# One prefill kernel on one core: a new bank for a piece of the early carry, and a new order for the first third of the tasks

## The chip, the cores and the metric

One core of a Trainium2 chip runs the whole program. The time is the device time of one execution in microseconds (us), as a median over runs. The core has five instruction streams that run beside each other and meet only at semaphores: TensorE (PE, matrix products), VectorE (DVE), ScalarE (ACT), GpSimd (POOL) and SyncE (SP, which here issues nearly all the transfers). Matrix products end in PSUM, which has eight banks; all other data lie in SBUF.

## The reference, cut to what matters

```python
def _attn_ref(q, k, v, alpha):            # each (4, 8, 768, 48)
    state = zeros((B, H, D, D))
    for t in range(S):
        state = alpha[:, :, t, :, None] * state + einsum('bhd,bhe->bhde', k[:, :, t], v[:, :, t])
        y[:, :, t] = einsum('bhd,bhde->bhe', q[:, :, t], state)

def _moe_ref(x, w_gate, w_val, w_out):    # x (3072, 384); weights (384,1536), (384,1536), (1536,384)
    g = x @ w_gate
    return (g * (1 / (1 + exp(-g))) * (x @ w_val)) @ w_out
```

The output of the first function, with the eight heads side by side in each row, is the `x` of the second.

## The kernel before, in words

**The two halves.** The recurrence is cut into 16 units of 192 positions, four to a batch, and the second half into seven blocks of tokens (384 or 512), each with 12 steps f over the hidden width. A step s is three long PE tasks: `g` (gate), `v` (value) and `o` (out). Each product is done with high and low parts of both factors, so `g` is nine matmuls. Block 0 needs the outputs of units 0 and 1, block 1 those of units 2 and 3. Steps 0 to 6 are block 0, steps 7 to 13 block 1 with the same weights.

**One unit.** Alpha, k and q arrive in rows (`La`, `Lk`, `Lq`). For the first four units they are copied into one of two wide buffers (`pa`, `pk`, `pq`, line 366), turned by PE into two PSUM banks (`Ta`, `Tk`, `Tq`, line 378) and taken from there (`ea`, `ek`, `cq`, line 927, or directly by the next multiplication). A backward running product of alpha (`G`, line 429) is multiplied by k (`mk`, line 953), a forward one (`f`, lines 433 and 436, in place in the single tile `AT`) by q (`q`, line 453 out of PSUM or 455 out of SBUF; `qc` copies a part of it, line 461). The keys are turned back (`K`, line 482; `kc`, lines 486 and 487), the scores are products of keys and queries (`S`, line 523), masked by `ma` (line 621). `Bw` (function `carry`, line 599) makes the state carried from chunk to chunk; `ad` copies it out (lines 635 and 642), `de` decays it into the next unit (line 650), `vc` copies values (line 468). `Y` (lines 693 to 710) gives the unit's output in two banks; `yh` and `yl` cut it into high and low parts (lines 724 and 728). For units 0 and 1 PE lays it out for the blocks (`R`, line 758; `x`, line 762); for the others ten to twelve transfers do (`xr`, line 775).

**Weights.** They come as 64-bit numbers in groups of one piece (groups 0 to 2) or two (all others): `wl` loads, `wNv0` to `wNv2` make single precision out of the words (lines 70 to 88), `wNa` and `wNp` make the high and low part (lines 291 and 295). Group 0 is the gate piece of step 0, group 1 its value piece, group 2 the gate of step 1, then in turn two of the list.

**The order.** Nothing is scheduled at run time. The string `ORDER` lists all tasks as `engine:name` (t PE, v DVE, s ACT, g POOL, y SP), with the PSUM banks of a task behind `@`. Each engine runs its own tasks strictly in this order, and waits at a task whose data, tile or bank is not yet free. A bank is free when the last reader of its former tile is done. The eight digits name A0, A1, A2, ops0, ops1, vps, gps, ops2; 6 is the bank of every `g` and 5 that of every `v`.

In `carry`, one piece of what is carried, `beside`, lies in the free columns of the first bank of the scores of the same unit:

```python
beside = st["S"][0][:, GF * T : GF * (T + D)].rearrange("p (g e) -> p g e", g=GF)
```

Of the kernel before, what the change touches and what calls it, by code (L numbers as in the profile page):

```python
# [28 lines left out]

WIDE = [(u + x, i) for u in range(0, NPE, 2) for x, i in ((0, 0), (1, 0), (0, 2), (0, 1), (1, 1), (1, 2))]  # L30
# [1229 lines left out]
```

## Time and profile before

| what | us |
|---|---|
| time of three runs, median | 550.85 |
| lowest and highest | 550.74, 550.98 |
| span of the profiled execution, first to last instruction | 549.9 |
| PE busy in it | 531.2 |
| start of the first `g` | 45.42 |

The profile is that of one execution. It shows its span; its own time with what lies around the span is not shown, and the median is 0.95 us longer than the span. Busy time is the time in which an engine runs an instruction; a row of a timeline has the start, the duration from the first to the last of the merged instructions, and in brackets how long the engine sat idle before and what ended the wait. The first 85 us matter here: before 45.42 us PE has only small tasks, and after it the long products run.

### The profile page before, as it was taken

How to read it: one execution, taken by the hardware profiler on the slowest of the kernel's cores; microseconds unless marked ns; L12 is line 12 of the kernel's file. 1: busy time of each engine (PE TensorE's matmuls, PEld its weight loads, DVE VectorE, ACT ScalarE, POOL GpSimd, SP SyncE). 2: the span in 40 equal slices, each digit the busy share in tenths (PEclk: the TensorE clock that was granted, in tenths of full speed). 3: DMA queues.
4: the chain of work that ended last, by engine and by line, in shares of the span. 5: the costliest groups of instructions: out<-in, count | busy, mean ns of one | idle time of the engine just before them, and what ended most of it. 6: DMA issues, size and time to landing. Idle time of an engine off the chain costs nothing.

```text
span 549.9 us, 13452 instructions
## 1 busy us (share of the span) xinstructions
PE 531.2 (97%) x5365; PEld 477.5 (87%) x5365; DVE 387.7 (71%) x619; ACT 264.1 (48%) x568; POOL 129.6 (24%) x139
## 2 busy tenths in 40 slices
PE   5879999999999999999999999999999999999995
PEld 3769999999999999998888888888888888899994
DVE  6989899998898997987789856476968353212122
ACT  5778754245334335423423513343335475447691
POOL 5454344142440122110202321012100030011011
PEclk9989999999999999999999999999999999999999
DMA  8889557574455656535464543546246434355321
GB/s 228 245 232 261 159 149 230 132 217 139 125 147 148 162 141 169 174 97 127 139 162 118 129 125 67 135 116 157 54 113 152 99 99 110 95 155 126 103 65 49
DMA packets 115111, 77.66 MB, mean 141 GB/s; under 512 B 53728, under 2 KB 111968, under 8 KB 115040
## 3 DMA queue, kind: packets, MB, share of 16 engines
q1 hardware_dynamic: 114192, 75.98, 51.9%
q8 instruction: 44, 0.72, 0.6%
q10 hardware_dynamic: 848, 0.74, 0.4%
q14 instruction: 27, 0.22, 0.2%
HBM read 62.52 MB, written 5.90 MB: 124 GB/s over the span
## 4 chain that ended last, share of the span: by engine, by line
PE 94%; DVE 2%; ACT 1%; DMA 1%; POOL 0%; issue 0%; DVEq 0%; POOLq 0%; ACTq 0%
PE g L791 27%; PE v L791 27%; PE ops L847 14%; PE ops L842 14%; PE y L680 3%; PE s L551 2%; PE A L599 1%; PE A L559 1%; PE pt L378 1%; PE kps L482 1%; DVE Gs L429 1%; DMA Le<-in_alpha_dram 1%; PE s L523 0%; ACT AT L927 0%; DVE t L78 0%; PE y L710 0%
## 5 line engine op out<-in xcount | busy, mean ns | idle before, releaser
L791 PE MATMUL g<-xT,w 128*128 128x384 f32 (+1 forms) x756 | 163.4, 360 | 0.0
L791 PE MATMUL v<-xT,w 128*128 128x384 f32 (+1 forms) x756 | 162.8, 359 | 0.0
L791 PEld LDWEIGHTS v<-xT,w 128*128 128x128 f32 x756 | 136.1, 188 | 13.2
L791 PEld LDWEIGHTS g<-xT,w 128*128 128x128 f32 x756 | 135.9, 188 | 13.2
L803 DVE TENSOR_TENSOR h<-h,v 128x384 f32<-128x384 f32 (+1 forms) x84 | 51.2, 609 | 110.6 <-PE v L791 94.3
L814 POOL TENSOR_TENSOR hl<-h,hh 128x384 fp32r<-128x384 f32 (+1 forms) x44 | 50.4, 1146 | 267.0 <-ACT hh L808 250.1
L799 ACT ACTIVATE h<-g 128x384 f32<-128x384 f32 (+1 forms) x84 | 45.0, 536 | 137.7 <-PE g L791 119.7
L808 ACT CAST hh<-h 128x384 fp32r<-128x384 f32 (+1 forms) x84 | 46.6, 555 | 77.6 <-PE ops L842 35.3
L847 PE MATMUL ops<-w,hh 128*128 128x384 f32 x286 | 79.6, 337 | 0.0
L842 PE MATMUL ops<-hh,w 128*128 128x512 f32 x216 | 72.2, 393 | 0.0
L498 DVE STREAM_TRANSPOSE K<-Gs 32x384 f32<-32x384 f32 x96 | 54.7, 570 | 2.0
L847 PEld LDWEIGHTS ops<-w,hh 128*128 128x128 f32 x286 | 52.2, 188 | 0.4
L842 PEld LDWEIGHTS ops<-hh,w 128*128 128x128 f32 x216 | 40.5, 188 | 8.9
L847 PE MATMUL ops<-w,hl 128*128 128x384 f32 x143 | 47.8, 335 | 0.0
L842 PE MATMUL ops<-hl,w 128*128 128x512 f32 x108 | 42.2, 391 | 0.0
L295 POOL TENSOR_TENSOR w<-t,w 128x768 fp32r<-128x768 f32 (+1 forms) x16 | 30.5, 1907 | 34.5 <-ACT w L291 30.8
L814 DVE TENSOR_TENSOR hl<-h,hh 128x384 fp32r<-128x384 f32 (+1 forms) x40 | 26.8, 670 | 8.9 <-ACT hh L808 8.6
L429 DVE TENSOR_TENSOR_SCAN Gs<-AT,Z 128x776 f32<-128x776 f32 x16 | 28.3, 1770 | 4.2 <-ACT AT L927 4.1
L436 DVE TENSOR_TENSOR_SCAN AT<-AT,Z 128x774 f32<-128x774 f32 x16 | 29.9, 1868 | 0.6
L261 ACT ACTIVATE wc<-wc 128x384 f32<-128x384 f32 x36 | 19.9, 553 | 15.6 <-DMA wc<-in_moe_w_gate_dram 8.1
L847 PEld LDWEIGHTS ops<-w,hl 128*128 128x128 f32 x143 | 26.9, 188 | 0.0
L621 DVE TENSOR_TENSOR X<-s,mask 128x384 f32<-128x384 f32 (+1 forms) x36 | 19.3, 552 | 8.6 <-PE s L551 8.1
(140 smaller groups left out, 695.2 us busy)
## 6 DMA issues: line engine op xcount, KB each, us to landing
xT<-X SPq DMA_DIRECT2D x72, 72.0 KB, 2.2
raw<-in_moe_w_gate_dram SPq DMA_DIRECT2D x12, 384.0 KB, 5.0
raw<-in_moe_w_val_dram SPq DMA_DIRECT2D x12, 384.0 KB, 6.2
V<-in_v_dram SPq DMA_DIRECT2D x96, 48.0 KB, 3.3
raw<-in_moe_w_out_dram SPq DMA_DIRECT2D x12, 384.0 KB, 4.7
wc<-in_moe_w_gate_dram SPq DMA_DIRECT2D x12, 384.0 KB, 3.7
wc<-in_moe_w_out_dram SPq DMA_DIRECT2D x12, 384.0 KB, 3.6
wc<-in_moe_w_val_dram SPq DMA_DIRECT2D x12, 384.0 KB, 4.2
```

The lines of the kernel that those rows point to most:

```text
L261: nc.scalar.activation(dev, dev, AF.Abs, accum_out=wviol[:, 1, i : i + 1])
L295: eng.tensor_tensor(out=lo, in0=src, in1=hi.bitcast(F32), op=ALU.subtract)
L429: nc.vector.tensor_tensor_scan(Gf[:, ::-1], Af[:, ::-1], Z[:, : 0 : -1], 0.0, op0=ALU.mult, op1=ALU.add)
L436: nc.vector.tensor_tensor_scan(Af, Af, Z[:, 1 : n + 1], Z[:, 0:1], op0=ALU.mult, op1=ALU.add)
L498: nc.vector.transpose(out=bass.AP(k0.tensor, k0.offset, [k0.ap[0], (G * 2 * D, NU), (2 * D, G), (1, 32)]), in_=Kg[j * BO + x : j * BO + x ...
L791: nc.tensor.matmul(pt, wsp[kind, f][a][:, kt * P : (kt + 1) * P], xT[blk][:, b_, kt, :], start=(n == 0), stop=(n == 3 * KT - 1),)
L799: nc.scalar.activation(h, acc.pop(("g", blk, f)), AF.Silu)
L803: nc.vector.tensor_tensor(out=h, in0=h, in1=acc.pop(("v", blk, f)), op=ALU.mult)
L808: nc.scalar.copy(out=hh, in_=acc["h", blk, f])
L814: eng.tensor_tensor(out=hl, in0=acc.pop(("h", blk, f)), in1=hh.bitcast(F32), op=ALU.subtract)
L842: nc.tensor.matmul(ops[blk][i], wsp["o", f][a][:, i * P : (i + 1) * P], h[b_], start=(first and n == 0), stop=(last and n == 2),)
L847: nc.tensor.matmul(ops[blk][i], h[b_][:, i * P : (i + 1) * P], wsp["o", f][a], start=(first and n == 0), stop=(last and n == 2),)
```

## The change

The order of the tasks is new from the start up to about step 41; from there on (about two thirds of the program) the string is the same. Engines change for some tasks, of which these matter here. From ACT to POOL go the wide copies `pa0`, `pk2`, `pa3`, `pk3`, `pq3` and the copies `qc0` to `qc2`; from POOL to ACT `pk0`, `vc1`, `w3a`, `w4a`; from POOL to DVE `mk1` and `w4p`; from DVE to POOL `q3`; from DVE to ACT `w0a` and `w4v0`; from ACT to DVE `ad2.2`, `w8v0` and a few more late ones. The numbers of the banks are new for nearly all early tasks. In `carry` the piece `beside` gets a PSUM tile of its own in a second bank, named in the order (`Bw0@73`). The wide buffer that was read longest ago is picked, where a list fixed the pair. `decay` names its tile directly. `NPE` is split in two names of the same value, 4, which changes nothing; those lines and the last two functions of the diff are left out here, and the order is shown up to `g7`.

```diff
-
-WIDE = [(u + x, i) for u in range(0, NPE, 2) for x, i in ((0, 0), (1, 0), (0, 2), (0, 1), (1, 1), (1, 2))]
+NST = 4
...
 ORDER = """
-g:im g:is y:La0 g:ik s:pa0 y:La1 t:Ta0@51 y:Lq0 g:iv y:wl2 s:ea0 s:pq0 t:Tq0@52 v:G0 y:Lk0 v:f0 s:w2v0 s:pa1 v:q0 g:z0 y:Lk1 v:w2v1 t:Ta1@73 y:wl1 s:pk1 y:Lq1 s:ea1 t:Tk1@07 y:V0.1 y:V0.2 y:wl0 y:V1 v:G1 g:pk0 t:Tk0@16 s:w1v0 s:ek1 v:mk0 s:qc0 v:f1 g:mk1 s:pq1 y:La2 t:Tq1@30 v:w1v1 y:La3 s:cq1 y:V0 t:K0.1@4 s:w0v0 t:S0@35 s:kc0.1 v:w0v1 t:K0.2@1 t:K0.0@7 s:pa2 g:q1 s:kc0.2 v:ma0.2 t:Ta2@04 s:kc0.0 y:Lq2 g:z1 v:ma0.1 v:ma0.0 s:ea2 v:w0v2 s:pa3 t:Bw0@1 v:ad0.0 s:qc1 t:K1.2@0 s:ad0.2 y:Lk2 t:S1@63 v:w1v2 v:w0a g:w0p v:G2 v:w2v2 t:K1.1@5 g:ib y:V1.2 t:K1.0@2 s:kc1.2 s:ad0.1 s:pq2 t:Ta3@41 v:ma1.2 y:wl3 y:V1.1 v:f2 s:vc0 s:w2a s:kc1.0 v:de1 t:Y0@70 t:Tq2@32 v:ma1.1 s:yh0.0 s:kc1.1 g:w2p s:yh0.1 v:ma1.0 y:Lk3 v:q2 y:wl4 y:V2.2 g:w1a g:vc1 v:yl0.0 y:wl8 t:Bw1@2 v:ad1.0 s:pk2 v:yl0.1 v:w4v0 s:w3v0 y:Lq3 s:ad1.1 v:w3v1 y:V2.1 v:w3v2 s:ad1.2 s:ea3 t:Y1@50 g:w1p v:w4v1 y:wl7 t:Tk2@14 t:R0.0@2 s:yh1.0 v:w4v2 s:yh1.1 g:w4a y:wl6 v:yl1.0 v:yl1.1 t:R0.1@3 g:w4p t:R1.2@5 s:qc2 s:x0.0 v:z2 y:V2 s:x0.1 t:R0.2@3 s:pk3 s:x0.2 v:mk2 s:pq3 s:x1.2 t:R1.0@1 t:S2@72 v:G3 t:Tk3@60 t:K2.2@4 t:R1.1@3 v:ma2.2 y:wl5 s:x1.0 v:mk3 t:K2.0@2 y:V3.2 t:Tq3@50 s:kc2.2 s:x1.1 t:K3.0@3 y:wl9 s:w6v0 y:V3.1 v:ma2.1 v:ma2.0 s:kc2.0 y:V3 s:cq3 t:g0 t:v0 g:w3a v:f3 v:q3 s:sl0 v:de2 s:w5v0 g:w3p v:w5v1 t:K2.1@2 s:kc2.1 s:w7v0 s:qc3 y:Lk4 v:w6v1 t:S3@46 v:w5v2 t:K3.1@0 v:ma3.2 y:La4 v:w6v2 s:w5a t:Bw2@2 v:ad2.0 v:h0 v:ma3.1 t:K3.2@1 t:g1 t:v1 s:kc3.1 y:wl11 s:ad2.2 v:ma3.0 s:kc3.0 v:de3 v:w7v1 s:sl1 t:g2 v:h1 s:ad2.1 g:w5p v:w7v2 t:Bw3@0 v:ad3.0 s:vc2 t:Y2@27 s:hh1 s:ad3.1 y:wl10 s:hh0 s:yh2.0 s:yh2.1 g:w6a v:hl1 v:w7a s:w9v0 v:w6p s:sl2 v:yl2.0 v:yl2.1 t:v2 g:hl0 t:o0 v:h2 s:vc3 v:w9v1 s:w8v0 v:w9v2 v:w8v1 g:w7p s:w10v0 g:z3 s:hh2 t:g3 y:wl12 v:w8v2 s:sl3 s:w8a t:v3 t:Y3@02 v:w10v1 v:w10v2 s:yh3.0 t:o1 t:g4 v:h3 s:yh3.1 v:tr4 g:w8p v:yl3.1 t:v4 g:hl2 s:w9a s:w10a y:xr2 s:hh3 v:yl3.0 s:sl4 y:wl13 v:tk4 t:o2 v:hl3 t:g5 v:h4 v:w9p s:w11v0 s:sl5 s:hh4 s:w12v0 v:G4 s:kc3.2 y:V4 t:o3 t:v5 v:hl4 g:w10p v:w11v1 y:xr3 v:h5 v:mk4 v:kr4.0 t:g6 y:Lq4 t:o4 v:w11v2 v:w12v1 v:w11a y:wl14 s:hh5 g:hl5 t:v6 s:sl6 t:g7
+g:im g:iv y:La0 g:ib g:pa0 t:Ta0@10 g:ik s:ea0 v:G0 y:Lq0 y:La1 s:pq0 s:pa1 y:Lk0 y:Lk1 y:Lq1 t:Tq0@57 t:Ta1@61 v:f0 v:q0 v:z0 s:pk0 s:pk1 t:Tk0@20 v:mk0 g:is t:Tk1@53 y:wl1 y:La2 y:wl2 s:ea1 y:V0.2 t:K0.2@0 v:G1 s:pq1 s:ek1 t:K0.1@5 s:kc0.2 s:kc0.1 v:mk1 s:pa2 t:Tq1@20 v:f1 y:wl0 s:cq1 y:V0.1 g:qc0 s:w1v0 y:V0 t:S0@63 t:K0.0@0 t:Ta2@14 v:ma0.2 s:kc0.0 s:w0v0 v:ma0.1 v:ma0.0 s:w2v0 v:w0v1 t:Bw0@73 y:V1 y:Lq2 g:q1 s:ea2 s:vc0 v:w1v1 s:ad0.2 t:S1@16 v:z1 v:w2v1 v:w0v2 s:ad0.1 v:w2v2 v:G2 t:K1.1@4 t:K1.2@0 t:K1.0@3 y:V1.2 y:La3 y:V1.1 s:kc1.1 v:ma1.2 v:w1v2 g:w1a v:de1 t:Y0@74 s:kc1.0 y:wl3 g:qc1 y:Lk2 y:wl4 s:kc1.2 v:ma1.1 y:V2 g:w1p s:pq2 s:w2a g:pk2 s:w0a y:wl7 t:Bw1@23 s:yh0.1 s:vc1 v:ma1.0 t:Tq2@16 v:f2 s:yh0.0 g:pa3 g:w0p v:yl0.1 t:Tk2@40 s:w3v0 s:ad1.1 s:w4v0 v:q2 v:z2 t:Ta3@56 y:Lk3 v:yl0.0 v:mk2 s:ea3 v:w3v1 t:K2.2@1 g:qc2 s:ad1.2 v:w4v1 t:Y1@40 t:R0.1@3 t:R0.2@2 t:R0.0@6 s:yh1.1 s:yh1.0 s:kc2.2 v:G3 y:Lq3 v:yl1.1 t:S2@75 s:x0.0 y:V2.2 t:K2.0@1 v:yl1.0 t:R1.0@0 g:pk3 t:R1.1@4 v:ma2.2 s:x0.1 s:x0.2 v:w3v2 t:R1.2@5 g:pq3 t:Tk3@36 v:mk3 s:x1.1 t:K2.1@2 s:x1.2 s:x1.0 g:w2p s:kc2.1 s:w7v0 t:Tq3@43 s:cq3 y:V3 y:V2.1 s:kc2.0 t:v0 t:g0 v:f3 v:de2 s:sl0 y:wl5 s:w3a y:wl9 y:wl6 v:ma2.0 t:Bw2@24 s:vc2 v:ma2.1 g:q3 v:w4v2 g:w3p t:g1 v:h0 s:w4a v:ad2.2 v:w4p v:de3 v:w7v1 s:w5v0 v:w7v2 t:v1 s:qc3 s:sl1 v:h1 t:K3.0@6 s:ad2.1 s:w6v0 s:hh0 v:w5v1 v:hl0 y:V3.1 y:Lk4 s:hh1 v:w5v2 s:kc3.0 t:S3@13 t:K3.1@0 t:Y2@42 t:K3.2@7 s:w5a v:z3 t:g2 t:v2 v:w6v1 v:w6v2 s:kc3.1 s:kc3.2 y:V3.2 t:Bw3@7 s:sl2 s:yh2.1 s:yh2.0 g:w5p v:ma3.2 v:h2 y:wl8 v:w6a v:yl2.0 v:yl2.1 g:w6p y:wl11 v:ma3.0 s:ad3.1 t:g3 v:w8v0 v:ma3.1 s:vc3 y:wl10 t:o0 v:w8v1 t:Y3@20 t:v3 s:w7a v:w7p s:hh2 s:w9v0 g:hl1 s:sl3 t:g4 t:o1 v:w9v1 v:h3 v:w8v2 y:xr2 s:yh3.1 s:yh3.0 s:w8a s:w10v0 t:v4 g:hl2 s:hh3 v:w9v2 y:wl12 v:w8p v:w10v1 s:sl4 s:w9a y:La4 y:V5.2 v:hl3 s:w11v0 v:yl3.0 t:g5 g:w9p v:h4 v:yl3.1 t:o2 s:w12v0 s:sl5 t:o3 s:hh4 v:w11v1 v:w10v2 v:hl4 t:v5 s:w10a v:tr4 y:xr3 g:w10p v:h5 v:G4 y:wl14 y:Lq4 v:w12v1 t:o4 t:g6 y:V5 v:w11v2 v:w12v2 t:v6 s:sl6 v:h6 v:w11a s:hh5 t:g7
...
 def main_path(ctx, tc, q, k, v, alpha, w_gate, w_val, w_out, out, flag, spill):
...
+    wide_read = list(range(-NP, 0))
...
     def widened(u, i, L, eng):
 
-        Wd = state[u]["wide", i] = Wide[:, WIDE.index((u, i)) % NP]
+        w = min((x for x in range(NP) if wide_read[x] is not None), key=lambda x: wide_read[x])
+        wide_read[w] = None
+        Wd, state[u]["wide", i] = Wide[:, w], w
...
     def pe_transposed(u, i, banks):
 
-        Wd = state[u].pop(("wide", i))
-        r = []
+        w = state[u].pop(("wide", i))
+        Wd, r = Wide[:, w], []
...
+        wide_read[w] = max(-1, *(x for x in wide_read if x is not None), -1) + 1
         return r
...
-    def carry(u, bank, whole=False):
+    def carry(u, bank, bank2, whole=False):
...
-        beside = st["S"][0][:, GF * T : GF * (T + D)].rearrange("p (g e) -> p g e", g=GF)
+        beside = None
+        if bank2 is not None:
+            beside = ps.tile([P, GF * D], F32, tag=bank2, name=f"A3_{u}").rearrange("p (g e) -> p g e", g=GF)
...
     def decay(u, eng):
...
-                out=state[u]["V"][r, 0, :, VC[j]], in0=SE[r], scalar=1.0 / FRAME,
+                out=Vt[u % NV][r, 0, :, VC[j]], in0=SE[r], scalar=1.0 / FRAME,
...
-            todo[f"Bw{u}"] = lambda eng, bank: carry(u, bank, True)
+        if u < NST:
+            todo[f"Bw{u}"] = lambda eng, bank, bank2=None: carry(u, bank, bank2, True)
```

## Rows read from the trace of the kernel before

**Rows 1.** Page of the profile, first part: busy us by engine.

```profile
PE 531.2 (97%) x5365; PEld 477.5 (87%) x5365; DVE 387.7 (71%) x619; ACT 264.1 (48%) x568; POOL 129.6 (24%) x139
```

**Rows 2.** Windows: stretch, length, busy us by engine, clock, transfer share, GB/s.

```profile
0.00:45.42 45.42, 33.25 (x537) 28.14 (x537) 37.83 (x54) 32.08 (x73) 24.34 (x44) 0.96 0.87 240
45.42:84.70 39.28, 39.28 (x476) 37.96 (x474) 36.20 (x48) 25.78 (x54) 13.00 (x11) 1.00 0.65 184
84.70:543.50 458.80, 458.70 (x4358) 411.44 (x4357) 313.13 (x518) 206.22 (x442) 92.25 (x84) 1.00 0.49 129
```

**Rows 3.** Waits of PE, 0 to 80 us: us in total, times, longest.

```profile
PE A L599 <- DVE X L453: 2.1, 1, 2.1
PE s L599 <- DVE X L621: 0.7, 1, 0.7
```

**Rows 4.** Windows, the stretch in which PE's clock was low (columns as in rows 2).

```profile
32.20:36.70 4.50, 3.84 (x74) 3.59 (x74) 4.43 (x7) 1.13 (x4) 0.20 (x1) 0.62 0.97 286
```

**Rows 5.** Timeline of PE.

```profile
32.24 0.38 PE L599 MATMUL A<-V,K 128*48 128x96 f32 x4 [2.06 <-DVE X L453]
...
39.29 1.30 PE L758 MATMUL xp<-Y,sel 112*128 112x384 f32 x6
...
42.59 0.87 PE L378 MATMUL pt<-ident,wide 128*128 128x128 f32 x6
...
45.42 1.81 PE L791 MATMUL g<-xT,w 128*128 128x384 f32 x9
...
84.52 1.72 PE L791 MATMUL g<-xT,w 128*128 128x384 f32 x9
```

**Rows 6.** Timeline of DVE.

```profile
6.82 1.77 DVE L429 TENSOR_TENSOR_SCAN Gs<-AT,Z 128x776 f32<-128x776 f32 x1 [3.80 <-ACT AT L927]
...
8.85 1.83 DVE L436 TENSOR_TENSOR_SCAN AT<-AT,Z 128x774 f32<-128x774 f32 x1
...
15.46 2.42 DVE L436 TENSOR_TENSOR_SCAN AT<-AT,Z 128x774 f32<-128x774 f32 x1
17.81 2.48 DVE L78 SCALAR_TENSOR_TENSOR t<-raw,t 128x384 uint32<-128x384 uint32 x2
20.22 1.58 DVE L621 TENSOR_TENSOR X<-s,mask 128x384 f32<-128x384 f32 x3
21.82 1.03 DVE L88 SCALAR_TENSOR_TENSOR t<-raw,t 128x384 uint32<-128x384 uint32 x2
...
28.48 1.50 DVE L650 SCALAR_TENSOR_TENSOR V<-SE,Gs 48x192 f32<-48x192 f32 x2
...
31.15 1.03 DVE L453 TENSOR_TENSOR X<-pt,AT 112x384 f32<-112x384 f32 x2
...
34.47 0.96 DVE L88 SCALAR_TENSOR_TENSOR t<-raw,t 128x768 uint32<-128x768 uint32 x1
...
43.21 1.02 DVE L953 TENSOR_TENSOR Gs<-pt,Gs 128x384 f32<-128x384 f32 x2
...
48.29 0.73 DVE L650 SCALAR_TENSOR_TENSOR V<-SE,Gs 48x192 f32<-48x192 f32 x2
```

**Rows 7.** Timeline of POOL.

```profile
11.49 1.30 POOL L366 COPY wide<-Le 128x576 f32<-128x576 f32 x1 [0.65 <-ACT wide L366]
14.57 1.69 POOL L956 TENSOR_TENSOR Gs<-trk,Gs 128x768 f32<-128x768 f32 x1 [1.78 <-DVE Gs L429]
18.03 1.85 POOL L455 TENSOR_TENSOR X<-trq,AT 112x768 f32<-112x768 f32 x1 [1.77 <-DVE AT L436]
...
31.39 1.00 POOL L295 TENSOR_TENSOR w<-t,w 128x384 fp32r<-128x384 f32 x1
```

**Rows 8.** Timeline of ACT, one wide copy.

```profile
10.35 0.67 ACT L366 COPY wide<-L 128x576 f32<-128x576 f32 x1 [0.58 <-DMA L<-in_k_dram]
```

**Rows 9.** Timeline of SP, the transfers that lay out unit 3.

```profile
72.11 7.44 SPq L775 DMA_DIRECT2D xT<-X  x10
```

**Rows 10.** Page, sixth part: transfers by issue, count, size, median us to landing.

```profile
xT<-X SPq DMA_DIRECT2D x72, 72.0 KB, 2.2
```

More of the change, by code (lines that the diff above doesn't have):

```diff
@@ L342, in load_t @@
             return L
-        L = Lt[(i + NPE // 2) % NL]
+        L = Lt[i % NL]
         Lv = L.rearrange("r (g x) -> r g x", g=G)
@@ L465, in values_copied @@
         Vd = state[u]["V"]
-        g0 = 0 if u >= NPE else GF
+        g0 = 0 if u >= NST else GF
         for j, r in ((0, slice(BO, P)), (1, slice(0, BO))):
@@ L538, in scores_carry @@
         if not last_of_batch(u):
-            if u > NPE:
+            if u > NST:
                 beside = state[u - 1]["beside"]
@@ L617, in causal @@
         r, z, f = (
-            (slice(0, P), 1, 0) if u >= NPE else (slice(BO, P), 0, 0), (slice(0, BO), 1, 0), (slice(0, P), 1, 1)
+            (slice(0, P), 1, 0) if u >= NST else (slice(BO, P), 0, 0), (slice(0, BO), 1, 0), (slice(0, P), 1, 1)
         )[i]
@@ L715, in rows_hi @@
     def rows_hi(u, i):
-        if i == 0:
-            st = state[u]
+        st = state[u]
+        if "Y" not in st:
             st["Y"] = st["X"] if u >= 2 else p2.tile(
@@ L728, in rows_lo, with swapped @@
         nc.vector.tensor_tensor(out=lo, in0=yps, in1=hi.bitcast(F32), op=ALU.subtract)
+    def swapped(u, g):
+        return g % 2 if u >= NST else g == G - 1
     def yrow(u, h):
-        return ((h + (h // 2 % 2 if u >= NPE else h // 2 == G - 1)) % 2) * BO
+        return ((h + swapped(u, h // 2)) % 2) * BO
     xT = {}
@@ L757, in pe_repack @@
             c0 = SEL + kt * P - 2 * D * g
-            nc.tensor.matmul(xp, sels[g == G - 1][:, c0 : c0 + P], Y[:, :, g, :], start=(n == 0), stop=(n == len(gs) - 1))
+            nc.tensor.matmul(xp, sels[swapped(u, g)][:, c0 : c0 + P], Y[:, :, g, :], start=(n == 0), stop=(n == len(gs) - 1))
     def x_copied(u, kt, copy):
@@ L964, in named_unit @@
         todo[f"q{u}"] = lambda eng: qhat(u, eng)
-        if u < NPE:
+        if u < NST:
             todo[f"qc{u}"] = lambda eng: q_odd(u, eng)
@@ L976, in named_unit @@
             todo[f"kr{u}.{i}"] = lambda eng, i=i: k_rows(u, i)
-            if i < 3 and (i != 1 or u < NPE):
+            if i < 3 and (i != 1 or u < NST):
                 todo[f"ma{u}.{i}"] = lambda eng, i=i: causal(u, i)
         todo[f"de{u}"] = lambda eng: decay(u, eng)
-        todo[f"S{u}"] = lambda eng, *banks: (scores if u < NPE else scores_carry)(u, banks)
-        if u < NPE:
-            todo[f"Bw{u}"] = lambda eng, bank: carry(u, bank, True)
-        todo[f"Y{u}"] = lambda eng, *banks: (outputs if u < NPE else outputs_quarters)(u, banks)
+        todo[f"S{u}"] = lambda eng, *banks: (scores if u < NST else scores_carry)(u, banks)
+        if u < NST:
+            todo[f"Bw{u}"] = lambda eng, bank, bank2=None: carry(u, bank, bank2, True)
+        todo[f"Y{u}"] = lambda eng, *banks: (outputs if u < NST else outputs_quarters)(u, banks)
         for kt in range(KT):
```

2 lines of the change are left out of this document (1 added, 1 removed).

## The prediction

> **What bounds the kernel now.** I read the page's shares first: PE is busy 531.2 of 549.9 us, DVE, the next, 387.7 [rows 1]. Windows cut at the first `g` show where the idle time lies: PE is busy 33.25 of the first 45.42 us, so 12.2 us idle; from there to 84.70 all of the time; and then 458.70 of 458.80 up to 543.5 [rows 2]. After 45.42 the program is PE's own work without a gap. So the change, which leaves PE's products alone, can win only by starting `g` and `v` of step 0 earlier, and keeps what it wins only if nothing makes PE wait later.
>
> The second thing to read is who is full before that. DVE is busy 37.83 of 45.42 us, nearly all of what is left after its first scan can start at 6.82 [rows 2, 6], and PE's two stalls at line 599 both end with a DVE instruction: 2.1 us on `q2` before `Bw1`, 0.7 us on a mask before `Bw0` [rows 3]. The head of the kernel is DVE's lane. Beside that PE's clock falls: right after the 2.06 us of idling it stands at 0.62 of full over 4.5 us, a mix of the 1.2 and the 2.4 GHz level, with 3.84 us of PE work in it [rows 4, 5].
>
> **The change, part by part.** *The own bank.* `beside` leaves the first score bank. Before, `Bw0` must wait until all masks of unit 0 have read both score banks; that is the wait of 0.7 us [rows 3]. Now it waits for the first mask only (`ma0.2`, which empties bank 3). Below, 0 if the keys' copies end last, as I find; above, 0.7 us.
>
> *Bw1 before Tq2, other banks.* Before, `Tq2` holds bank A2, so `Bw1` waits for `q2`, far down DVE's queue. Now `Bw1` takes banks 2 and 3, freed by ACT's copies, and precedes `Tq2`. The 2.1 us stall [rows 3] goes; what is late next is `Y1`, behind `Tk2` and so behind `mk2` on DVE (it wants banks 4 and 0). If the stall goes and the clock stays up, the 3.84 us of PE work cost 3.84 x 0.38 = 1.5 us less at most [rows 4]; nothing if other gaps, which I expect, pull the clock down again.
>
> *DVE's lane, which I take as the path.* In the new order, up to `mk3`, on which the last early transposition (`Tq3`, ahead of `v0` on PE) depends for a bank. `pa0` moves to POOL: 1.30 us where ACT takes 0.67 [rows 7, 8], but POOL copies the first half while the second waits its turn, so I let `G0` start at 7.0 instead of 6.82. Prices, start to start: a scan 1.8, a forward scan with its reciprocal 2.06, a pair out of PSUM (`q`, `mk`, `yl`) 1.02, a mask 0.53, a word instruction on one piece 0.5 and on two 0.95, `de` 0.75, a two-input product in SBUF 0.96 by the word instruction of the same size [rows 6].
> G0, f0, q0, mk0, G1, mk1, f1: 1.8 + 2.06 + 1.02 + 1.02 + 1.8 + 0.96 + 2.06 = 10.7, so 17.7; before, `f1` ends at 17.88 [rows 6]: no gain yet, since `mk1` on DVE eats what the lost collision gives back.
> Three masks 1.6, five word instructions 2.5: 21.8. G2 1.8, a mask 0.5, a word instruction 0.5, `de1` 0.75, two masks 1.1, f2 2.06: 28.5. Half of `yl0`, q2, the other half, mk2: 3.05, so 31.6. w3v1, w4v1 1.9, G3 1.8, both halves of `yl1` 1.02: 36.3.
> Then PE lays out unit 1: three `R` pieces of two matmuls, 1.2 (six matmuls took 1.30 [rows 5]), 37.5; `Tk3` 0.87 [rows 5], 38.4 (a mask and `w3v2` lie beside that on DVE, until 37.8); mk3 1.02, 39.4; half of `Tq3`, 0.4: `v0` at about 40. Before, `g0` started at 45.42 with one `K` piece more and one other less done, which is even. So 5.4 us are the most that this lane gives.
> Rougher sums of the same kind on ACT and PE (with the prices of the same tasks before) bring `Bw0` to 18.5, `Y0` to 24.4, `Bw1` to 26, `Y1` to 32.7; each then waits on ACT's copies or, from `Tk2` on, on DVE. ACT is relieved, on balance, of four wide copies of 0.67 [rows 8] and keeps up.
>
> *What POOL does to DVE.* The sum has no collision in it. The rows have: `f1` took 2.42 beside POOL's product of 14.57, against 1.83 for `f0`; two word instructions took 2.48 beside POOL's `q1`, against 1.03 alone; `de1` 1.50 against 0.73 [rows 6, 7]. Where DVE reads PSUM there was none: `q2` took 1.03 with POOL's 1.00 us product inside it [rows 6, 7]. In the new order `q1` lies beside the masks, which read PSUM, but between 24 and 38 us POOL has w1a, w1p, pk2, pa3, w0p, pk3, pq3, w2p: by the rows of 1.30 and 1.00 some 8.8 us (the cast `w1a` and the three products of one piece at 1.00 or a bit less). Below, 0: all of them meet DVE at PSUM. Above, 8.8: each holds DVE up for its whole length. Before, these three collisions cost 0.6 + 1.45 + 0.77 = 2.8 us, and 12 of the lane's 21 us between 17.7 and 39.4 read SBUF alone. I take 2.0, nearer the lower end since a POOL task can as well be the one held up. `v0` then starts at 42, 3.4 us earlier than `g0` did.
> The Trainium skill ("SBUF — State Buffer", section "Who interferes with whom") calls this an exclusive lock on a shared port pair: the later of the two waits for the whole of the other, and only DVE instructions with two SBUF inputs, or in a fast mode, take part. By that, which engine loses depends on who starts first, and the five wide copies given to POOL speak against the change: they would price it at the upper end. The rows above agree as far as they go; none has a wide copy beside a DVE instruction with two SBUF inputs, so the price of the copies by that rule is not shown here.
>
> *Transfers.* `q` of unit 0 is loaded before alpha of unit 1, and `k` and `q` of the first two units before `wl1`. No term changes by it. New is that `V2` and `V3` stand on SP in front of other loads: `V2` waits for `Y0`, `V3` for `Y1`, and behind them stand `wl7`, `Lk3`, `Lq3`, and `V2.1`, `wl5`, `wl9`, `wl6`. Here `Y0` ends near 26 and `Y1` near 34.5; `Lk3` then comes in time for `pk3` only just. I put 0 to 1 us on it, inside the 2.0.
>
> *After v0.* Unit 3's layout on SP waits for `yl3` on DVE. Before, it started at 72.11, 27.9 us after `mk3` was done at 44.23 [rows 6, 9]; the tasks that the new order puts between the two on DVE also add up, at the same prices, to 27.9 us, to which I add 1.3 for collisions as above. With `mk3` done at 39.4 + 2.0 = 41.4 the layout starts at 70.6, ten transfers take 7.44 us and land 2.2 after issue [rows 9, 10], so 80.2. `g7`, which reads it, stood at 84.52 [rows 5] and would now stand at 81.1. That leaves 0.9 us, so of the 3.4 I give 0.4 to waits of this kind between 42 and 81 us. What is won at `g7` stays, because PE ran without a gap behind it and the order there hardly differs.
>
> *Sum.* 5.4 - 2.0 - 0.4 = 3.0 us from a span of 549.9: 546.9. The median of the runs is 0.95 us above this span; added, 547.9, rounded to 547.8.
>
> **The rivals.** *All of it.* Collisions cost nothing and the clock stays up: 5.4 us, to which the clock can add up to 1.5. 550.85 - 5.4 = 545.4, down to 544.0. For it: POOL's heavy tasks could fall on DVE's PSUM reads. Against: the rows show three collisions in the same 15 us.
> *Given back.* `v0` starts 2 to 5 us early, but DVE, busy 36.20 of 39.28 us after it [rows 2], does not follow: PE waits for weights or for unit 3's transfers at `g7`, since the lane from `mk3` to `yl3.1` is no shorter than before. If collisions there cost 3 us instead of 1.3 the gain falls to about 1: 549.8 to 551.9 hold this case. For it: the equal sums. Against: the sum above still has 0.9 us to spare at `g7`.
> *Slower: POOL holds DVE.* One mechanism, between 24 and 38 us: the wide copies and products of POOL hold DVE's SBUF instructions. It decides once they cost more than the 5.4 us: 5.4 + 1.1 to 8.8 give 552.0 to 554.3. For it: 1.45 us lost beside a single POOL task. Against: half of the lane reads PSUM.
> *The change does not do what it says.* The own bank buys nothing by itself, since `Bw0` waits for the last copy of the keys; this is in the sum at 0, and would leave the forecast as it is.
>
> **How the numbers follow.** The forecast (546.5 to 549.6) has 0.47, all of it (544.0 to 546.5) 0.20, given back within 0.2% 0.17, slower 0.16. About 0.2%, 1.1 us, is what a measurement of this kernel can tell from no change. Faster: 0.67; same: 0.17; slower: 0.16. The range leaves out little more than the slower case and the very best: 544.3 to 551.3. For the likeliest case alone it is 546.5 to 549.6.
>
> **What would show it right or wrong.** In the profile of after: the first long product at 40 to 43 us; `Bw1` without a wait on DVE; DVE nearly full from 7 us to there, with some scans or word instructions stretched past 2.3 and 0.9 us beside POOL's copies; PE without idle time from `v0` on but for at most half a microsecond at `g7`. It is wrong if the first long product stands later than 44 us, if PE waits more than 1.5 us after it, or if the lane's stretched rows add up to more than 4 us.

## The result, and the profile after

| | median us | lowest to highest | runs |
|---|---|---|---|
| before, beside the changed kernel | 550.91 | 550.74 to 552.16 | 4 |
| changed | 554.46 | 553.78 to 554.89 | 4 |

The ratio of the times is 1.0058 (95% interval 1.0042 to 1.0075): slower by some 3.2 us, where 547.8 was forecast, and outside the range. The profiled execution took 554.71 us, with a span of 553.0 against 549.9 before. In every run that gives both, an execution takes 1.7 to 1.8 us more than its span. By that the profiled execution of the kernel before took some 551.6 us (an estimate), 0.7 above the median, and leads read from its trace can be too large by as much.

The start of the long products came as forecast: the first of them, now `v0`, starts at 41.73 us (forecast 42; 45.42 before [rows 5]). The loss lies behind it. Windows of the changed kernel, columns as in [rows 2], in the last row PE alone; 278.86 is the start of `g42`, by which PE has done the same products in both orders:

```profile
0.00:41.73 41.73, 29.65 (x536) 25.39 (x537) 33.21 (x52) 29.64 (x70) 21.66 (x41) 1.00 0.76 209
41.73:84.70 42.97, 42.58 (x490) 40.61 (x489) 40.83 (x56) 27.31 (x53) 18.64 (x12) 1.00 0.67 197
84.70:200.00 115.30, 114.01 (x1232) 109.90 (x1232) 106.82 (x162) 42.11 (x90) 49.25 (x44) 1.00 0.66 173
200.00:300.00 100.00, 97.71 (x1098) 86.51 (x1097) 75.30 (x119) 34.30 (x77) 25.58 (x25) 1.00 0.47 123
...
41.73:278.86 237.13, 233.16 (x2546) 1.00 0.60 161
```

The same window of the kernel before, from its first `g` to `g42`:

```profile
45.42:275.17 229.75, 229.75 (x2546) 1.00 0.58 158
```

The same 2546 products took 229.75 us without a gap before, and 237.13 us after: 3.97 us of idling, and 3.4 us more that count as busy. Successive products overlap in the trace, so a wait leaves a gap that is too short, or none: start to start, the place with the gap of 1.31 us in front of `o34` lost 1.58. The lead of 3.7 us at `v0` becomes 3.7 us of arrears at `g42`. The first part of it goes early, since at `g7` the lead is 2.4:

```profile
82.09 1.72 PE L798 MATMUL g<-xT,w 128*128 128x384 f32 x9
```

Before, `g7` started at 84.52 [rows 5], and the products from the first long one to `g7` are the same: 40.36 us after, 39.10 before. From `g42` to the end the changed kernel is no slower (274.1 us against 274.7).

PE's waits in the whole changed kernel (in total, times, longest):

```profile
PE pt L380 <- POOL wide L368: 4.9, 2, 4.7
PE A L604 <- ACT t L69: 2.8, 1, 2.8
PE ops L854 <- POOL hl L821: 1.3, 1, 1.3
PE v L798 <- DVE h L810: 1.2, 3, 0.8
...
PE s L554 <- ACT h L806: 1.0, 1, 1.0
```

The first is nearly all the wait for the first data, 4.7 us in both kernels. The second lies ahead of `v0`, in the middle of `Bw1`. The timeline of PE there:

```profile
25.61 1.94 PE L604 MATMUL A<-V,K 128*48 128x96 f32 x48
30.32 0.65 PE L604 MATMUL A<-V,K 128*48 128x48 f32 x16 [2.77 <-ACT t L69]
...
41.73 1.83 PE L798 MATMUL v<-xT,w 128*128 128x384 f32 x9
```

`Bw1` stands still for 2.77 us after 48 of its 64 products, at its change to the second bank. The instruction named as the releaser is a word instruction that `Bw1` does not read; its keys had been copied by 25.33 us. So the name is no explanation, and the experiments come back to it.

The other three shown lie behind `v0` and are one pattern. The timeline of ACT near 238 us:

```profile
237.74 0.56 ACT L260 ACTIVATE wc<-wc 128x384 f32<-128x384 f32 x1 [5.50 <-DMA wc<-in_moe_w_out_dram]
...
239.73 0.47 ACT L806 ACTIVATE h<-g 128x384 f32<-128x384 f32 x1
```

that of DVE near 182 us, with `h25` behind the wait:

```profile
182.34 1.64 DVE L355 STREAM_TRANSPOSE AT<-L 128x768 f32<-128x768 f32 x1 [2.39 <-DMA L<-in_alpha_dram]
...
184.92 0.55 DVE L810 TENSOR_TENSOR h<-h,v 128x384 f32<-128x384 f32 x1
```

and that of POOL, behind ACT's delay:

```profile
240.73 3.50 POOL L821 TENSOR_TENSOR hl<-h,hh 128x384 fp32r<-128x384 f32 x2 [8.20 <-PE A L562]
```

`wc22` waits 5.50 us for its transfer at the head of ACT's queue, and `sl35`, which the scores of unit 9 wait for, stands behind it. `tr8` does the same to `h25` on DVE. `hl34` and `hl35`, on POOL in this order, take 3.50 us for two; `o34` waits for the first.

Collisions are read from DVE's timeline (the first row is a scan alone, for comparison; the last lies just behind `v0`, beside `q3` on POOL):

```profile
12.70 1.77 DVE L432 TENSOR_TENSOR_SCAN Gs<-AT,Z 128x776 f32<-128x776 f32 x1
...
24.31 0.92 DVE L655 SCALAR_TENSOR_TENSOR V<-SE,Gs 48x192 f32<-48x192 f32 x2
...
35.71 2.23 DVE L432 TENSOR_TENSOR_SCAN Gs<-AT,Z 128x776 f32<-128x776 f32 x1
...
43.54 2.14 DVE L655 SCALAR_TENSOR_TENSOR V<-SE,Gs 48x192 f32<-48x192 f32 x2
```

and from POOL's, with wide copies alone and beside DVE's work:

```profile
31.90 0.66 POOL L368 COPY wide<-L 128x576 f32<-128x576 f32 x1 [2.95 <-PE pt L380]
...
34.91 3.49 POOL L368 COPY wide<-L 128x576 f32<-128x576 f32 x2 [0.81 <-PE y L699]
```

The collisions stretch DVE's scan by 0.46 us and `de1`, two instructions, by 0.19 (0.92 against 0.73 [rows 6]); two copies of 0.66 take 3.49 together. It is mostly POOL that is held up.

### The profile page after: what moved, and what is told of

Its sections match the earlier page's. It is cut to its first block, busy times and chain, and to the rows that moved or that the text cites. A ratio compares the mean times of both kernels' runs of the same rounds, so it can differ in the third digit from the quotient of the medians.

```text
span 553.0 us, 13476 instructions
## 1 busy us (share of the span) xinstructions
PE 530.9 (96%) x5365; PEld 475.3 (86%) x5365; DVE 383.0 (69%) x617; ACT 256.1 (46%) x554; POOL 153.5 (28%) x155
## 4 chain that ended last, share of the span: by engine, by line
PE 82%; DVE 6%; DMA 4%; ACT 2%; issue 2%; SPq 2%; POOL 1%; DVEq 0%; POOLq 0%
PE v L798 24%; PE g L798 24%; PE ops L849 14%; PE ops L854 11%; PE y L685 3%; PE s L554 2%; PE A L562 1%; DMA L<-in_k_dram 1%; DVE K L501 1%; DVE Gs L432 1%; DMA L<-in_alpha_dram 1%; DVE AT L439 1%; DMA wc<-in_moe_w_out_dram 1%; DVE h L810 1%; SPq L401 1%
## 5 line engine op out<-in xcount | busy, mean ns | idle before, releaser
L821 POOL TENSOR_TENSOR hl<-h,hh 128x384 fp32r<-128x384 f32 (+1 forms) x55 | 69.0, 1257 | 280.6 <-ACT hh L815 260.9
L294 POOL TENSOR_TENSOR w<-t,w 128x768 fp32r<-128x768 f32 (+1 forms) x14 | 26.1, 1869 | 18.4 <-ACT w L290 17.0
L458 POOL TENSOR_TENSOR X<-trq,AT 112x768 f32<-112x768 f32 x10 | 17.0, 1701 | 33.4 <-DMA L<-in_alpha_dram 12.8
L821 DVE TENSOR_TENSOR hl<-h,hh 128x512 fp32r<-128x512 f32 (+1 forms) x29 | 19.1, 659 | 8.1 <-ACT hh L815 7.9
```

The lines of the kernel that those rows point to most:

```text
L294: eng.tensor_tensor(out=lo, in0=src, in1=hi.bitcast(F32), op=ALU.subtract)
L821: eng.tensor_tensor(out=hl, in0=acc.pop(("h", blk, f)), in1=hh.bitcast(F32), op=ALU.subtract)
```

## The experiments

The theories after this reading: **theory 1**, the order between `g7` and about step 41 loses what the head wins; **theory 2**, an earlier PE finds DVE and the transfers late in whatever order; and **theory F**, added after the first profiles, that the stall in `Bw1` is PE waiting for its own instructions. Executions of one kernel differ by up to 6 us in these groups, so ratios to the kernel before, run beside, are given. Diffs show words of `ORDER`.

**e1, e2: one order's head with the other's rest.** All tasks up to `g7` from one string, the rest in the sequence of the other:

```diff
-(after) ... v:w11a s:hh5 t:g7 g:hl5 v:tk4 s:sl7 s:hh6 t:v7 v:hl6 ...
+(e1)    ... v:w11a s:hh5 t:g7 y:wl13 v:tk4 y:V4 v:mk4 v:kr4.0 g:hl5 s:hh6 y:wl15 t:v7 y:V4.2 v:w11p s:sl7 ...
```

> The order of the changed kernel up to g7, then all tasks that are left in the order and on the engines of the kernel before. Theory 1 (the order between g7 and about step 41 loses what the head wins: tasks that wait for a transfer or run slowly on POOL stand right ahead of tasks that the next step needs): the 3.7 us of the earlier v0 are kept but for about half a microsecond, 547 to 548 us. Theory 2 (an earlier PE finds the other engines and the transfers late, whatever the order): the gain is given back, 550.3 to 551.5 us.

> The opposite: the order of the kernel before up to g7 (the piece beside in the score bank for these units), then all tasks that are left in the order of the changed kernel. Theory 1: the middle loses its 5 to 7 us from a start that is not earlier, 556 to 558 us. Theory 2: the middle lost only because PE came early, and with the old head it waits less, 551 to 553 us.

Measured: e1 552.08 us, ratio 1.0013 (0.9992 to 1.0035); e2 568.55, ratio 1.0305. Neither theory had e1's number. Its `v0` starts at 39.21, 6.2 us ahead of the kernel before; at `g8` the lead is still 4.4, and then it goes at one place:

```profile
PE ops L854 <- DVE w L294: 2.8, 1, 2.8
```

`o5` waits for `w11p`, since the seam has put 7 us of DVE work between `h6` and `h7`; PE's clock falls behind it (granted 0.83 from 80 to 100 us). From `g9` to the last `g` the arrears stay between 1.5 and 1.3 us, so the old order loses nothing, but there was no lead left to keep. In e2 the seam is worse (6.0 us of waiting at one `o`), and it tells nothing between the theories.

**e3: the own bank taken away.** `Bw0@73`, `Bw1@23`, `Bw2@24` become `Bw0@7`, `Bw1@2`, `Bw2@2`, `beside` is again in the score bank, and

```diff
-s:ad1.1 s:w4v0 ... s:ea3 v:w3v1 t:K2.2@1 g:qc2 s:ad1.2
+s:ad1.1 s:ad1.2 s:w4v0 ... s:ea3 v:w3v1 t:K2.2@1 g:qc2
```

> The changed kernel with the piece beside back in the score bank for units 0 to 2 and each Bw on its first bank alone; ad1.2 stands right behind ad1.1, since Tq2 now waits for it. Theory A (the own bank buys nothing, as in the prediction): Bw0 starts within 0.2 us of where it does, v0 within 0.5 us, 554 to 555 us. Theory B (the own bank carries part of the earlier start): Bw0 waits up to 0.7 us for the last mask, or Tq2 for the copy of the carry, v0 is 1 to 2 us later, 555 to 556.5 us.

Measured: 559.5 us, ratio 1.0152 (1.0124 to 1.018), against 1.0064 for the changed kernel in e5: 5 us worse, more than either theory gave. PE's waits:

```profile
PE s L604 <- issue: 1.7, 1, 1.7
PE s L604 <- DVE X L626: 1.7, 2, 0.9
PE pt L380 <- ACT SE L647: 1.6, 1, 1.6
```

The first is the stall in `Bw1` again, shorter than in the changed kernel's first profile (2.77). The second are `Bw0` and `Bw2` waiting for masks, the third `Tq2` waiting for the copy of the carry. `v0` starts at 44.11, 2.4 us later than in that profile although the stall is 1.1 us shorter. In this order, which was made for it, the own bank is worth about 5 us.

**e4: one word moved.**

```diff
-y:wr22 s:wc22 s:sl35 t:v35 t:o33 v:h35 t:S9@162 v:G10 y:xr8.0 s:hh34 s:hh35
+y:wr22 s:sl35 t:v35 t:o33 v:h35 t:S9@162 v:G10 y:xr8.0 s:hh34 s:hh35 s:wc22
```

> The changed kernel with one word moved: wc22, which waits 5.5 us on ACT for its transfer ahead of sl35, stands behind hh35. Theory 1: the stall of 1.2 us at S9 goes, and of the 1.6 us at o34 the part that comes from hh34 being late, so 1.2 to 2.8 us less, 551.7 to 553.3 us. Rival: the stall moves to the next task that needs the weight or to POOL's hl34, and nothing or less than 0.5 us is won, 554 to 554.5 us.

Measured: 551.09 us, ratio 1.0006 (0.9984 to 1.0028). The waits at the scores of unit 9 (1.0 us) and at `o34` (1.3) are gone from the trace; one of 0.8 for a transfer of `x` came at 245 us. That is how theory 1 has it. The ratio fell by 0.5% or 3 us, below theory 1's range and more than the two waits account for; the scatter told of below is as large as the rest.

**e5: the changed kernel again.**

> The changed kernel as it is, once more, beside the others of this group. In its first profile Bw1 stands still for 2.8 us at 27.6 us although its data are there, and PE goes on 1.7 us after a 16 KB packet of the queue of instructions has ended; in the first experiment, whose order is the same up to there, that packet came 4 us earlier and v0 started at 39.1 instead of 41.7 us. Theory F (the late packet decides): executions fall in two groups about 3 us apart, some near 551.5 and some near 554.5, and a profile of the lower group has no stall at Bw1. Rival: the stall belongs to the order (a transfer or a wait that the profile does not show), and all executions lie at 553.8 to 555 us.

Measured: 554.16 us (551.60 to 556.96), ratio 1.0064 (1.0039 to 1.009): spread, but not in two clean groups. The profiled execution is the fastest, and its `Bw1` has no stall:

```profile
25.53 2.29 PE L604 MATMUL A<-V,K 128*48 128x96 f32 x64
...
39.18 1.83 PE L798 MATMUL v<-xT,w 128*128 128x384 f32 x9
```

Its lead of 6.2 us at `v0` is gone at the end too (span 549.9 as before): 6 us are lost behind `v0`.

**e6, e8, e14, e17: transfers around 22 us.** e6 moves the load of group 4 back, e8 is e6 with e7's edit; e14 (on e13) moves that of group 3 ahead; e17 moves that of group 7, which stood further back, ahead of that of group 4.

```diff
-y:wl3 g:qc1 y:Lk2 y:wl4 s:kc1.2 v:ma1.1 y:V2
+(e6)  y:wl3 g:qc1 y:Lk2 s:kc1.2 v:ma1.1 y:V2 y:wl4     with s:w4v0 behind s:ad1.2, v:w4v1 behind v:yl1.0
+(e17) y:wl3 g:qc1 y:Lk2 y:wl7 y:wl4 s:kc1.2 v:ma1.1 y:V2
-y:V1 y:Lq2
+(e14) y:V1 y:wl3 y:Lq2
```

> The changed kernel with the load of weight group 4 behind V2 on SP, and with its first two word tasks moved as much (w4v0 behind ad1.2 on ACT, w4v1 behind half of yl1 on DVE), so that 0.4 MB less stand in the transfer queues when PE wants the packet of instructions at 23 us. Theory F: the packet comes before 25 us, Bw1 runs through, v0 starts at 38.5 to 39.5 us, and nearly all executions lie in the lower group, 551 to 552 us. Rival (the stall belongs to data, or the load that is later makes other tasks late): the stall stays or comes back at step 2, 554 us or more.

> Both edits in one kernel: the moved tasks of the middle and the later load of group 4. Theory F with theory 1: 547 to 548 us in nearly all executions, faster than before and after. If only the first holds, 550.5 to 552; if only the second, 550 to 551; if neither, 553 us or more.

> The changed kernel with the load of weight group 7 ahead of that of group 4 on SP, so that 0.8 MB more stand in the transfer queues at 22 to 27 us. Theory F (the packet of PE's instructions waits behind queued transfers): the packet starts at 27 to 30 us, Bw1 stands still between its 48th and 49th product in the profile until 2.7 us after the packet's start, 3 us or more, and hardly an execution is below 553 us. Rival (a wait of Bw1 for its second bank): the stall doesn't grow with the transfers, 0 to 3 us as in the other profiles.

> The same, and the load of weight group 3 between V1 and Lq2 on SP, about 5 us earlier, when the transfer queues are less full, so that they hold 0.4 to 0.8 MB less when PE wants its packet at 22 us. Theory F (queued transfers make the packet late): hardly an execution has the stall at Bw1, the spread of 5 us shrinks to 2 us, median 546.5 to 548 us. Rival (the packet is late for another reason, or Lq2 and what follows come later by as much): the spread stays at 4 to 5 us and the median within 0.5 us of the run without this.

Measured: e6 553.63 us, ratio 1.0043 (1.0027 to 1.0059); e8 551.43, 1.0012; e17 555.07 (552.50 to 558.08), 1.0077, with no stall in the profile, whose execution was the fastest and whose packet started at 22.78, the earliest of all; e14 548.09 (547.15 to 549.39), 0.9953. Only e14 has a smaller spread, 2.2 us against 4.7 in e13, at no lower median; it still has a stall of 0.84. So the transfers queued at 22 us are not shown to make the packet late. What the profiles do show is how the stall follows the packet, over runs whose PE instructions are the same up to there (16 KB packets of the queue of instructions, times in us; 705 is the count in the trace, weight loads included):

| run | packet starts | instruction behind the 705th starts | from packet to it | idle in `Bw1` |
|---|---|---|---|---|
| e7 | 22.91 | 27.15 | 4.24 | none |
| e13 | 23.38 | 27.21 | 3.83 | none |
| e5 | 24.76 | 27.18 | 2.42 | none |
| e8 | 25.36 | 27.98 | 2.62 | 0.58 |
| e14 | 25.75 | 28.30 | 2.55 | 0.84 |
| e10 | 26.76 | 29.38 | 2.62 | 1.95 |
| e4 | 27.05 | 29.90 | 2.86 | 2.38 |
| after | 27.59 | 30.32 | 2.73 | 2.77 |

A packet by 24.8 us costs nothing; each later one holds PE until 2.5 to 2.9 us after its start. The six other profiles with these instructions (e1, e6, e9, e17 without a stall, e11 and e12 with one) fit both. `v0` starts at 38.8 to 39.7 in the runs without a stall, and 41.7 to 42.6 in those with 2 us or more.

The scatter has a second part, PE's granted clock. In the changed kernel's first profile it stayed at 1.00 behind the stall of 2.77 us; in e4, behind one of 2.38, it was 0.57 from 30 to 34 us, a mix near the lower of its two levels (1.2 of 2.4 GHz). The first 42 us of the two (after, e4):

```profile
0.00:42.00 42.00, 29.92 (x538) 25.66 (x539) 33.44 (x53) 29.91 (x71) 21.66 (x41) 1.00 0.77 210
0.00:42.00 42.00, 30.98 (x532) 27.33 (x533) 33.50 (x51) 29.35 (x68) 22.58 (x41) 0.96 0.76 207
```

The kernel before shows it best: of its 120 executions beside these experiments the 42 with a mean granted clock of 0.998 or more took 549.7 to 551.5 us, the 18 with 0.991 or less 551.9 to 553.2.

**e16, e18: is the place counted in instructions?** Products of the identity ahead of the first transposition, 44 in e16, 6 in e18 (which is e17 otherwise); each is two matmuls and two weight loads:

```diff
+            if u == i == hf == 0:
+                for _ in range(44):
+                    nc.tensor.matmul(out=pt[:, 0, 0:8], lhsT=ident, rhs=ident[:, 0:8], start=True, stop=True)
```

> The changed kernel with 44 small products (128 x 8) of the identity in front of the first transposition, into a tile that the transposition overwrites, while PE waits for the first wide copy anyhow: 88 more instructions in front of all others. Theory F (PE stands where a block of 256 of its instructions begins and the packet with it is late): the place moves 88 instructions forward in the program, to the first products of Bw1, some 1.7 us earlier; no stall is left at the old place; the time is that of the changed kernel, 551.5 to 555 us. Rival (the stall belongs to the product it stands in, its operands or bank): it stays where it is in the program, in the middle of Bw1.

> The same, and 12 products of 128 x 8 of the identity (24 instructions) in front of the first transposition, while PE waits for the first wide copy. Theory F: the stall lies 12 products earlier in Bw1, between its 36th and 37th product, with none between the 48th and 49th. Rival (the second bank): it stays between the 48th and the 49th product.

Measured: e16 568.36 us; its products took 18.94 us, far more than the wait that they were to fill, the transfers were over by then, and no stall is left: nothing is told apart. e18 took 556.01, and its profile decides:

```profile
1.84 2.73 PE L381 MATMUL pt<-ident 128*128 128x8 f32 x12 [1.84 <-POOL ident masks.py:199]
...
25.46 1.56 PE L607 MATMUL A<-V,K 128*48 128x96 f32 x36
29.94 1.03 PE L607 MATMUL A<-V,K 128*48 128x48 f32 x28 [2.92 <-issue]
```

With 12 matmuls more in front, `Bw1` stands still after 36 of its products instead of 48, for 2.92 us, and goes on 2.63 us after its packet starts. A wait for the second bank would have stayed at 48. Theory F holds for the place.

**e7, e11: the middle mended.** Four tasks that wait for transfers move back, two `hl` go to DVE; e11 also moves `tk8` behind `h26`.

```diff
+s:sl25 s:wc2   +v:h25 v:tr8   +s:hh27 s:wc9   +s:hh34 v:hl34 v:G10 s:hh35 s:wc22   +v:ma9.2 v:hl35
```

> The changed kernel with tasks that wait for a transfer moved behind tasks that the next product needs: wc22 behind hh35, wc2 behind sl25, wc9 behind hh27 on ACT, tr8 behind h25 on DVE; and hl34 and hl35 on DVE, ahead of G10 and behind ma9.2, instead of on POOL. Theory 1 (the order after v0 loses the gain): the stalls at steps 26, 27, 34 and at the scores of unit 9 go, 0.9 + 0.4 + 1.6 + 1.2 = 4.1 us in the first profile, so 550 to 551 us in executions whose Bw1 stands still and 547 to 548 in those where it does not. Theory 2 (PE meets DVE full whatever the order): the stalls move to other tasks of DVE, and less than 1.5 us is won, 553 us or more (550 in the others).

> The kernel with the mended middle, and tk8 behind h26 on DVE, since there v27 now waits 1.5 us for h26 behind G8 and tk8. Theory 1: the 1.5 us go, 549 to 550 us as a median and 547.3 us where the packet is in time. Rival: the wait moves to h27 or to the keys of unit 8, less than 0.5 us.

Measured: e7 551.05 us (548.85 to 554.51), ratio 1.0003 (0.9981 to 1.0025), 3.1 below e5, which ran beside it, as theory 1 has it. Of PE's waits behind `v0` one is left above half a microsecond:

```profile
PE v L798 <- DVE h L810: 1.6, 2, 1.4
```

Even so the lead in this trace falls from 5.3 us at `g7` to 2.3 at `g42`: these moves don't mend all of the middle. e11 takes the wait of 1.4 away (0.3 us left) but measured 551.50, ratio 1.0008 (0.9986 to 1.003): not to be told from e7. Its profiled execution had a late packet.

**e9, e10, e13: the old rest, with better seams.** e10 goes over to the old order at `g12`. e9 is e1 with `tk4`, `mk4`, `kr4.0` behind `h7` and `f4` behind `h8`; e13 is e9 with

```diff
-v:w15v0 t:g9 t:v9 s:hh8 s:sl9 v:w15v1 v:hl8 t:g10 v:h9
+t:g9 t:v9 s:hh8 s:sl9 t:g10 v:h9 v:w15v0 v:w15v1 v:hl8
```

> The first experiment again (new head, then the order of the kernel before) with its seam mended: there DVE had 7 us of tasks between h6 and h7, so that v8 came 3 us late and the lead of 5 us was gone; here tk4, mk4 and kr4.0 stand behind h7 and f4 behind h8. Theory 1 (what is won at g7 stays with the old order): v8 waits less than 1 us, and the lead of 4 to 5 us of g9 is there at the end, 546 to 548 us. Theory 2 (DVE cannot be earlier than in the kernel before, so any lead is lost again): the lead is lost at another task before step 20, 550 to 552 us.

> The order of the changed kernel up to g12, and from there the tasks that are left in the order and on the engines of the kernel before. At this seam DVE has at most half a microsecond of work more or less than in the kernel before. Theory 1: nothing is lost after g12; with v0 at 38.6 to 39.1 us (no late packet) 545 to 547 us, with v0 at 41.7 some 548 to 550. Theory 2: PE waits for DVE or transfers between steps 13 and 40, 550 to 552 us.

> The kernel with the new head, the old rest and the mended seam, with h9 on DVE ahead of w15v0, w15v1 and hl8, since v10 waited 1.7 us for h9. Theory 1: that wait goes and nothing takes its place, the lead at the end grows from 3.4 to about 5 us in the profile without a late packet, 546 us, and the median falls to 548 to 549 us, 0.3 to 0.5% below the kernel before. Rival (DVE is behind by as much at the next step): v11 or o7 waits instead, median 550 to 551 us.

Measured: e9 550.45 us (lowest 547.64), ratio 0.9982 (0.9963 to 1.0002); e10 550.22, 0.9994; **e13 547.32 (546.75 to 551.43), ratio 0.9958 (0.9938 to 0.9978)**, faster than both kernels. e9's lead of 5.4 us at `g9` fell to 3.4 at one wait for `h9` and then stayed, between 3.4 and 3.6, from `g12` to the last `g`. e10 had a late packet and lost 2.7 us at its seam, and keeps 1.0 to 1.1 from there. e13's windows (its `v0` starts at 39.28):

```profile
39.28:84.70 45.42, 45.04 (x504) 43.08 (x503) 43.15 (x58) 28.23 (x55) 21.21 (x15) 1.00 0.70 202
84.70:200.00 115.30, 114.92 (x1246) 111.96 (x1246) 107.16 (x167) 45.67 (x93) 32.79 (x29) 1.00 0.62 167
200.00:300.00 100.00, 100.00 (x1103) 87.88 (x1102) 85.34 (x129) 39.10 (x87) 19.79 (x19) 1.00 0.54 141
```

Theory 1 is shown: with the rest in the old order PE idles 0.76 us from `v0` to 300 us. Of the 6.1 us by which `v0` is early, 4.9 are left at `g7`, 3.9 behind the seam, and 3.9 to 4.0 from there to the last `g` (the spans, 545.2 against 549.9, differ by 4.7; the medians by 3.2). Theory 2 falls.

**e12: POOL's wide copies back on ACT.** `g:pa0`, `g:pk2`, `g:pa3`, `g:pk3`, `g:pq3` become `s:`.

> The changed kernel with the five wide copies pa0, pk2, pa3, pk3, pq3 on ACT, as before the change, in the same places of the order. The prediction gave 2.0 us to POOL holding DVE up before v0. If that is its price, DVE's rows before v0 get shorter by about 2 us, v0 starts up to 2 us earlier than at 38.6 (packet in time) or 41.7 us, and the time falls by up to 2. Rival A (the copies cost DVE next to nothing, under 0.5 us): v0 stays within 0.5 us, 553 to 555 us. Rival B (ACT becomes the late engine, 5 x 0.67 us more): v0 is 1 to 3 us later, 555 to 557 us.

Measured: 553.58 us, ratio 1.0039 (1.0017 to 1.0061), against 1.0064 for the changed kernel: within the scatter. `v0` starts at 42.63 behind a stall of 2.71 us and a fall of the clock (0.51 from 30.7 to 34.2 us), against 42.43 in e4, which has both too: no earlier. DVE's scan that took 2.23 us is back at

```profile
36.84 1.77 DVE L432 TENSOR_TENSOR_SCAN Gs<-AT,Z 128x776 f32<-128x776 f32 x1
```

and that half microsecond is most of what the copies cost DVE ahead of `v0`: rival A, with the scatter as a limit to what the time can tell.

**e15: the own bank alone,** in the kernel before: `Bw0@1` becomes `Bw0@12`, `Bw1@2` becomes `Bw1@25`.

> The kernel before with one part of the change: the piece beside of units 0 and 1 in a PSUM tile of its own (Bw0 on banks 1 and 2, Bw1 on 2 and 5); order and engines as before. By the prediction the bank alone buys 0 to 0.7 us: the wait of Bw0 for the last mask goes, 550 to 551 us. Rival: the wait for the mask hid another (the last copy of the keys, or K1.0 and Y1 now wait for the copy of the carry), and the time stays within 0.3 us or rises by up to 1 us.

Measured: 552.91 us, ratio 1.0044 (1.0024 to 1.0063): slower by 2.4 us, more than either expectation. The wait for the mask [rows 3] is gone, but:

```profile
PE A L604 <- DVE X L456: 2.2, 1, 2.2
PE y L698 <- ACT SE L647: 1.6, 1, 1.6
PE kps L485 <- issue: 1.4, 1, 1.4
```

`Y1` now waits 1.6 us for ACT's copy out of the bank (0.6 before), and the wait of `Bw1` for `q2` is still there. The last row is the wait for instructions, 0.4 us in the kernel before; so of the 1.3 us by which `g0` is later here (46.74) `Y1`'s wait brings 0.9 and a late packet, not the bank, 1.0, less the 0.7 of the mask. The mean granted clock was 0.984 to 0.995 in all nine executions, 0.988 to 0.999 in the kernel before. In the old order the bank gains nothing, since what it frees isn't next; how much of the 2.4 us it costs isn't shown.

## Why the prediction was wrong

**The step that failed** is "What is won at `g7` stays, because PE ran without a gap behind it and the order there hardly differs." PE's gapless 458.70 of 458.80 us [rows 2] belonged to the old order of the other engines, and that order differs up to step 41, as the section on the change says. From `v0` to `g42` the changed order lost 7.4 us: 1.3 up to `g7`, where the sum has 0.4, and 6.1 behind it, where the sum has nothing. In the trace `wc22`, `tr8` and POOL's `hl` stand ahead of what PE needs next (e4, e7), and with the old order in their place the lead stays (e9, e13). "PE waits more than 1.5 us after it" was named as what would show the prediction wrong; it waited 3.97.

**The start of `v0`: the right number by luck, from two wrong terms.** 42 was forecast and 41.73 came. In it are 2.77 us of waiting for instructions, which no term had, and collisions of about 0.7 us ahead of `v0` where 2.0 were taken. Without the late packet `v0` starts at 38.8 to 39.7, against "about 40" for DVE's lane without collisions: that sum was sound to about 1 us.

The prediction read the Trainium skill ("SBUF — State Buffer", section "Who interferes with whom") as pricing the copies at the upper end; by the page the order of issue decides which of the two waits. The rows agree that they exclude each other (two copies of 0.66 us took 3.49), and here it was POOL that waited, while DVE lost 0.5.

A row of the kernel before could have told. The prediction says that none has a wide copy beside a DVE instruction with two inputs in SBUF, but the 1.30 us that it takes as POOL's price of a copy is one. That copy ran from 11.49 to 12.79 [rows 7], and DVE's timeline has

```profile
11.72 0.55 DVE L78 SCALAR_TENSOR_TENSOR t<-raw,t 128x384 uint32<-128x384 uint32 x1
12.57 1.85 DVE L429 TENSOR_TENSOR_SCAN Gs<-AT,Z 128x776 f32<-128x776 f32 x1 [0.30 <-ACT AT L927]
```

There too the copy took twice its 0.66 us, and the scan 0.08 more than its 1.77.

**The own bank at 0.** Wrong for this order: taking it out costs 5 us (e3), since `Bw0`, `Bw2` and `Tq2` then wait for masks and for the copy of the carry. In the old order it gains nothing (e15). A part that is nothing by itself carried the order built on it.

**`Bw1` without a wait on DVE**: as forecast. PE's clock stayed at 1.00 up to `v0` in the profile, where other gaps were expected to pull it down as in [rows 4]; in e4, e11 and e12 it fell behind the stall in `Bw1` (to 0.51 to 0.57 over 3.5 to 4 us). Nor is the fall of [rows 4] the rule before: the profile with it has a mean clock of 0.996, one without it (the changed kernel's) 0.998, and 42 of 120 executions of the kernel before have 0.998 or more. At `g7` PE did not wait, and the transfers of unit 3 were in time; the 1.3 us went in short delays on the way (0.4 of it shown as idle).

**The rivals.** "Given back" had the right sign of the event and the wrong mechanism: it let DVE fall behind at `g7`, and gave 549.8 to 551.9. "Slower: POOL holds DVE" gave 552.0 to 554.3, near the result, but by a mechanism that cost DVE about 0.5 us by e12's rows. No rival had the loss where most of it was, between `g7` and `g42`.

**What stays open:** why the packet of instructions is late in some executions (e6 and e17 moved transfers and settled nothing, e14 only narrowed the spread), why the clock falls in some executions and not in others, and where e7's order still loses 3 us.

## What to carry to other kernels

When an order is rewritten over a stretch, cost the whole stretch: that PE had no gap there is a property of the other engines' old order, and an early start is lost at the first task that waits for a transfer at the head of an in-order queue with a needed task behind it. List, for each engine, the tasks that wait for a transfer and what stands behind them. To keep a part of a change that pays, join it to the old rest and look at the seam first: one 3 us wait there, and the fall of the clock behind it, hid a gain that a few moved tasks brought out (e1, e9, e13).
